# Clustered attention and two FFNs on one core: the weights' rounding moved behind the next gh, b made positive in the lead, the last pair's closing parts spread, the second FFN's outs three units behind

## The chip, the cores and the metric

The kernel runs on one core of a Trainium2 chip. The metric is the device time of one execution in microseconds (us); shown are three runs of the kernel before, of which the median counts. The trace is that of one further, profiled execution. The core's engines each work through their own instructions in order and wait for one another by semaphores: TensorE (PE, the matmuls), VectorE (DVE), ScalarE (ACT), GpSimd (POOL); SyncE (SP) issues the DMAs.

## The reference

Three computations in a row; all of it is in float32, and the weights come as float64.

```
q_assign = argmax(q_n . c_n); k_assign = argmax(k_n . c_n)      # cluster of each query and key, 16 clusters
scores   = q k^T / 8 where q_assign == k_assign, else -1e9
attn     = softmax(scores) v                                     # batch 2, 8 heads, seq 768, head_dim 64
x        = attn as 1536 tokens x 512

h = x @ w_in;  g = max(h, 0) + log1p(exp(-|h|));  x = g @ w_out  # first FFN, 512 -> 2048 -> 512

h = x @ w2_in                                                    # second FFN
g = (a0 + a1 h + a2 h^2 + a3 h^3) / (1 + |b0| |h| + |b1| h^2 + 1e-6)
out = g @ w2_out
```

## The kernel before

**Attention.** Two heads make a pair, and there are eight pairs (NP) with six tiles of 128 keys (NT). Pair 0 is prepared in a lead before the steps; step j then has PE compute the scores of pair j (tile `st`, L320 and L321), the row maxima of pair j+1 (`mxs`, L276), and attention times values (`av`). DVE reduces each `mxs` to a column of `mf` (L280); once six columns stand, PE transposes them (`nt`, L288), DVE makes the row `nr` (L290), and a DMA puts it beside the keys. ACT takes the exponential (`et`), POOL adds the tiles up (`ea`). What a step or the lead does comes from tables of positions (`AT`, `LEAD`): every piece is put on an axis with a number, and the pieces are issued by rising number. In the lead `coefficients` (position AB) issues the DMAs of `a_sb` and `b_sb`, the coefficients a and b of the second FFN.

The closing parts of a pair (`finish`) are 0: Ln and Exp of the sums on ACT, 1 to 3: three products on DVE (L385 to L389), 4: the rounding copy to `xh` on ACT (L394) and the rest `xl` on POOL. Those of the last pair run inside the first FFN.

**FFNs.** 1536 tokens make three blocks of 512; the hidden 2048 make 16 chunks of 128; one chunk for one block is a unit, so each FFN has 48 units, numbered 0 to 47 and 48 to 95. A unit is `g_in` (12 matmuls, L474 to L476, into one of four PSUM tiles `h`), the function on ACT and DVE, which leaves g split into a rounded part `gh` (ACT) and a rest `gl` (DVE, L530 or L532), and `g_out` (12 matmuls, called outs below, L545 to L547 or L549 to L551). Every product is three matmuls: high by high, high by low, low by high. The loop over units writes PE's order: outs(i) come one unit after g(i) in the first FFN and two units after it in the second, one more for a block's first chunk.

**Weights.** A chunk's float64 bits are loaded by one DMA (`stage_w`, 1 MB) and decoded by DVE in three passes (first L428, second L434, third L440); ACT rounds the result to `w` (L444, the cast), and DVE subtracts (L447, the rest). Cast and third pass are one piece. The loop takes four such pieces per unit in the first FFN's first block, so one chunk per unit, and from the second FFN's first unit on one piece per unit for the chunks 14 and 15 that are then left. The queue of pieces is served in order; `DE` puts the pieces of the first five chunks into the attention's last two steps (NP-2 and NP-1). At unit 3 ACT takes the absolute value of `b_sb` (L781), which needs its own activation table.

The first FFN's softplus and the Ln and Exp of attention and second FFN lie in different tables of ACT, which are loaded by ACT_TABLE_LOAD rows.

Of the kernel before, what the change touches and what calls it, by code (L numbers as in the profile page):

```python
# [10 lines left out]
F32 = mybir.dt.float32  # L11
# [17 lines left out]
DE = [  # L29
    [-11.7, -5.09, -3.77, -3.71],  # L30
    [-1.97, 0.49, 2.0, 0.04],
    [0.24, -2.3, -0.8, -0.33],
    [5.39, 3.04, 3.81, 10.72],
    [5.38, 8.42, 3.92, 3.46],
]
FN = [1.65, 2.38, 4.34, 7.01]
LEAD = dict(F1=[-0.92, -0.47], D=-8.72, E1=-2.11, E2=-1.3, OT=0.68, F2=[0.92, 3.97], F3=[3.64, 5.6], F4=[10.75, 6.7],
# [4 lines left out]
def clustered_attention_two_ffns(  # L42
# [372 lines left out]
    def decode_w(f, c):  # L415
# [35 lines left out]

        pieces.extend(((f, c), x) for x in (first, second, third, fourth))

    def run_pieces(n=0, upto=None):

        while pieces and (n > 0 or upto and pieces[0][0] <= upto):
            pieces.pop(0)[1]()
            n -= 1

# [116 lines left out]
    with tc.manual_schedule():  # L576
# [149 lines left out]
        nu = len(units)  # L726
        ahead = 2
        run_pieces(upto=units[0][::2])
        g_in(*units[0])
        av(NP - 1, NT - 1)  # L730
        run_pieces(upto=units[1][::2])
        g_in(*units[1])
        sums(NP - 1)
        att.close()
        pools["wb"] = ctx.enter_context(tc.tile_pool(name="wb", bufs=1))
        last = pools["wb"].tile([128, 2 * NW], F32R, tag=f"w{KF - 1}", name="last").bitcast(F32)
        last = last[:, 0:2 * S].rearrange("p (a n x) -> p a n x", a=2, n=2)
        evac_av(NP - 1, last[:, 0])
        evac_sums(NP - 1, last[:, 1])
        aps.close()  # L740
        pools["py"] = ctx.enter_context(tc.tile_pool(name="ps4", bufs=1, space=bass.MemoryType.PSUM))
        finish(NP - 1, 0)
        for c in range(8, KF - 1):
            stage_w(0, c)

        outs = [[] for _ in range(nu + 4)]
        for i, (f, blk, c) in enumerate(units):
            outs[i + (1, 2)[f] + (c == 0)].append((f, blk, c))
        F1 = NB * KF
        outs[F1] = outs[F1 - 1] + outs[F1]  # L750
        outs[F1 - 1] = []
        for i in range(nu + 3):
            u = units[i] if i < nu else None
            prev = units[i - 1] if 0 < i <= nu and units[i - 1][0] == 1 else None
            if u:
                if u[1] == 0:
                    run_pieces(upto=(u[0], u[2]))
                if i >= ahead:
                    g_in(*u)
                if i == F1:  # L760
                    nc.scalar.preload_act_table_set("natural_log_exp_and_others")
                act1(*u)
                if u[0] == 0:
                    g_hi(*u)
                    g_lo(*u)
            if prev:
                act3(*prev)
# [12 lines left out]
            if i == 3:  # L780
                nc.scalar.activation(out=b_sb, in_=b_sb, func=AF.Abs)  # L781
                stage_w(0, KF - 1)
                stage_w(1, 0)
            for f, c in ((0, i + len(DE)), (1, i - (NB - 1) * KF - 2)):
                if len(DE) * (f == 0) <= c < KF:
                    decode_w(f, c)
            run_pieces(1 if i >= F1 else 4)
            for o in outs[i]:
                g_out(*o)
                if o[:2] == (0, NB - 1) and o[2] < KF - 1:  # L790
                    stage_w(1, o[2] + 1)

# [41 lines left out]
```

## Time and profile before

| | us |
|---|---|
| median of three runs (824.18 to 826.26) | 824.36 |
| the profiled execution | 825.66 |
| its span in the trace | 823.9 |
| PE busy in the span | 782.0 (95%) |
| DVE busy | 597.9 (73%) |
| ACT busy | 441.5 (54%) |
| POOL busy, all of it before the FFNs | 185.5 (23%) |
| mean granted clock of TensorE | 0.979 of full speed |

A busy share is the mean over stages that have different limits: PE, DVE, ACT and POOL share the attention, and PE, DVE and ACT the FFNs. A full granted clock (1.0) is 2.4 GHz and 0.5 is 1.2 GHz; a value between is a mixture over the stretch. In the timelines a group of like instructions is one row with its count, the time in brackets is how long the engine stood idle before the row, and the name behind the arrow is what ended that.

### The profile page before, as it was taken

Reading aid. Unit: us, or ns where it says so; the run is one execution under the profiler, and the core shown is the slowest. Engines: PE = TensorE matmul, PEld = TensorE weight load, DVE = VectorE, ACT = ScalarE, POOL = GpSimd, SP = SyncE. Lnnn points to the kernel's source line nnn. Section 1 sums busy time; section 2 is a strip of 40 time slices with the busy share of each in tenths; the row PEclk is TensorE's granted clock in tenths of the full one; section 3 lists DMA queues with packets and bytes.
Section 4 is the critical chain, followed back from the end, with each engine's and each line's share of the span. In section 5 each row is a group of like instructions: output and inputs, shape, how many; then the busy total and the mean of one; then the engine's idle time right before and its main releaser. Section 6 shows DMA issues by size and latency. Waiting matters only on the chain.

```text
span 823.9 us, 9126 instructions
## 1 busy us (share of the span) xinstructions
PE 782.0 (95%) x3467; PEld 573.8 (70%) x3468; DVE 597.9 (73%) x759; ACT 441.5 (54%) x626; POOL 185.5 (23%) x103
## 2 busy tenths in 40 slices
PE   6799999999988899999999999979999999999997
PEld 3366565656555677788888887757788788887885
DVE  4888778887885878621112678889998798879886
ACT  3456666765474343331223333366777676667674
POOL 3375988898852000000000000000000000000000
PEclk9699999999999999999999999999999999999999
DMA  4553344424073520000000455410000100010001
GB/s 183 164 149 71 117 127 138 124 65 155 1 307 146 211 103 0 1 1 0 1 1 0 157 201 196 161 52 0 1 1 0 52 1 0 1 52 0 1 1 51
DMA packets 14635, 61.65 MB, mean 75 GB/s; under 512 B 3248, under 2 KB 4368, under 8 KB 10496
## 3 DMA queue, kind: packets, MB, share of 16 engines
q1 hardware_dynamic: 14176, 60.19, 21.7%
q10 hardware_dynamic: 416, 0.89, 0.3%
q8 instruction: 27, 0.44, 0.2%
q14 instruction: 16, 0.13, 0.1%
HBM read 49.32 MB, written 3.15 MB: 64 GB/s over the span
## 4 chain that ended last, share of the span: by engine, by line
PE 60%; DVE 23%; ACT 11%; issue 3%; DMA 2%; ACTq 0%; SPq 0%; DVEq 0%
PE av L342 7%; PE h L475 7%; PE h L476 7%; PE h L474 7%; DVE w L440 5%; PE yp L550 4%; PE yp L551 4%; PE st L320 4%; PE yp L549 4%; ACT w L444 4%; PE mxs L276 3%; PE st L321 3%; DVE w L434 3%; PE yp L546 3%; PE yp L547 2%
## 5 line engine op out<-in xcount | busy, mean ns | idle before, releaser
L476 PE MATMUL h<-xh,w 128*128 128x512 f32 x384 | 152.1, 396 | 0.5 <-DVE w L447 0.5
L474 PE MATMUL h<-xh,w 128*128 128x512 f32 x384 | 151.9, 396 | 0.3 <-ACT w L444 0.3
L475 PE MATMUL h<-xl,w 128*128 128x512 f32 x384 | 152.0, 396 | 0.0
L330 POOL TENSOR_TENSOR ea<-ea,et 128x768 f32<-128x768 f32 x60 | 117.8, 1981 | 24.1 <-ACT et L325 22.2
L280 DVE TENSOR_REDUCE mf<-mxs 128x1 f32<-128x768 f32 x96 | 87.6, 951 | 34.8 <-PE mxs L276 34.1
L530 DVE TENSOR_TENSOR gl<-y,gh 128x512 fp32r<-128x512 f32 x48 | 33.1, 691 | 102.6 <-ACT gh L522 102.6
L325 ACT ACTIVATE et<-st 128x768 f32<-128x768 f32 x96 | 73.3, 812 | 60.3 <-PE st L321 57.4
L444 ACT CAST w<-w 128x1024 fp32r<-128x1024 f32 x32 | 33.6, 1049 | 105.6 <-DVE w L440 105.6
L474 PEld LDWEIGHTS h<-xh,w 128*128 128x128 f32 x384 | 72.2, 188 | 19.0 <-issue 1.2
L476 PEld LDWEIGHTS h<-xh,w 128*128 128x128 f32 x384 | 72.1, 188 | 18.1 <-DVE w L447 1.0
L475 PEld LDWEIGHTS h<-xl,w 128*128 128x128 f32 x384 | 72.2, 188 | 17.1
L546 PE MATMUL yp<-gl,w 128*128 128x512 f32 x192 | 78.2, 407 | 4.3 <-DVE gl L530 3.9
L545 PE MATMUL yp<-gh,w 128*128 128x512 f32 x192 | 77.3, 403 | 4.6 <-issue 3.2
L549 PE MATMUL yp<-w,gh 128*128 128x512 f32 x192 | 77.1, 401 | 4.1 <-ACT gh L524 4.0
L550 PE MATMUL yp<-w,gl 128*128 128x512 f32 x192 | 77.7, 405 | 3.3 <-DVE gl L532 3.3
L547 PE MATMUL yp<-gh,w 128*128 128x512 f32 x192 | 76.7, 399 | 0.0
L551 PE MATMUL yp<-w,gh 128*128 128x512 f32 x192 | 76.4, 398 | 0.0
L320 PE MATMUL st<-qt,kt 128*128 128x384 f32 x192 | 70.7, 368 | 4.8 <-ACT et L325 2.4
L487 ACT ACTIVATE y<-h 128x512 f32<-128x512 f32 x48 | 28.5, 595 | 84.0 <-PE h L476 84.0
L342 PE MATMUL av<-et,vr 128*64 128x384 f32 x384 | 71.7, 500 | 1.0 <-ACT et L325 1.0
L321 PE MATMUL st<-qt,kt 81*128 81x384 f32 x192 | 65.7, 342 | 0.0
L447 DVE TENSOR_TENSOR w<-w,w 128x1024 fp32r<-128x1024 f32 x32 | 39.2, 1225 | 32.9 <-ACT w L444 32.9
(122 smaller groups left out, 1319.5 us busy)
## 6 DMA issues: line engine op xcount, KB each, us to landing
w<-in_moe_w SPq DMA_DIRECT2D x32, 1024.0 KB, 4.9
rawx<-in_x SPq DMA_DIRECT2D x7, 768.0 KB, 6.4
rawy<-in_y SPq DMA_DIRECT2D x7, 768.0 KB, 6.4
vr<-in_v SPq DMA_DIRECT2D x8, 384.0 KB, 6.0
kt<-kt SPq DMA_DIRECT2D x7, 384.0 KB, 4.0
out<-yo SPq DMA_DIRECT2D x9, 256.0 KB, 2.5
kt<-qt SPq DMA_DIRECT2D x7, 288.0 KB, 4.0
out<-y SPq DMA_DIRECT2D x3, 256.0 KB, 4.1
```

Source lines behind the costliest of these rows:

```text
L320: nc.tensor.matmul(t[:, n, 0:HS], lhsT=KT[j % 3][:, 0, h, c], rhs=QT[j % 3][:, 0, h, r], start=True, stop=False)
L321: nc.tensor.matmul(t[:, n, 0:HS], lhsT=KT[j % 3][0:RM + 1, 1, h, c], rhs=QT[j % 3][0:RM + 1, 1, h, r], start=False, stop=True)
L330: eng.tensor_tensor(out=ea[j, h], in0=et[j, 0, h] if kt == 1 else ea[j, h], in1=e, op=ALU.add)
L342: nc.tensor.matmul(av_t[j][64 * h:64 * h + 64, n, 0:HS], lhsT=VR[j % 2][:, h, kt, :], rhs=et[j, kt, h][:, n, :], start=kt == 0, stop=kt == ...
L474: nc.tensor.matmul(t, lhsT=wh[:, kk, :], rhs=h, start=kk == 0, stop=False)
L475: nc.tensor.matmul(t, lhsT=wh[:, kk, :], rhs=l, start=False, stop=False)
L476: nc.tensor.matmul(t, lhsT=wl[:, kk, :], rhs=h, start=False, stop=kk == KD - 1)
L546: nc.tensor.matmul(t, lhsT=wh[:, s], rhs=gl, start=False, stop=False)
L547: nc.tensor.matmul(t, lhsT=wl[:, s], rhs=gh, start=False, stop=last)
L549: nc.tensor.matmul(t, lhsT=gh[:, s], rhs=wh, start=first, stop=False)
L550: nc.tensor.matmul(t, lhsT=gl[:, s], rhs=wh, start=False, stop=False)
L551: nc.tensor.matmul(t, lhsT=gh[:, s], rhs=wl, start=False, stop=last)
```

## The change

Nothing that is computed changes. The closing parts, weights and units of both FFNs are put on one axis of positions, as the steps of the attention are, with a table `FT`. On it:

- The decode of a chunk has five pieces instead of four: the cast is its own piece, placed at 1.15 and the rest at 1.25 after the unit in which the three DVE passes stand, which is behind the next unit's `gh` and `gl`. In the second FFN the pieces of chunks 14 and 15 stand in two units each (`D2`).
- `b_sb` is made positive on DVE in the lead, right behind the issue of its DMA; ACT's Abs at unit 3 goes.
- Unit 1's `g_in` comes before unit 0's, both before the last `av` and the sums; the softplus of units 0 and 1 come before the last pair's Ln and Exp; the closing parts stand at positions 0.66, 1.12, 3.35, 5.33 and 9.13.
- The outs of the second FFN come three units behind, from its first chunk on.
- `DE` has five columns and other places.

```
 DE = [
-    [-11.7, -5.09, -3.77, -3.71],
...
+    [-11.88, -5.68, -3.02, -3.84, -4.46],
...
-FN = [1.65, 2.38, 4.34, 7.01]
+FT = dict(G=[-8.44, -11.09, 1.12], AV=-5.78, SM=-1.04, EV=[-1.36, -0.96], FN=[0.66, 1.12, 3.35, 5.33, 9.13],
+    A=[-0.02, 0.22, 1.25], L=[0.26, 0.77, 1.61], D2=[[51.2, 51.8, 52.2, 52.4, 52.8], [56.2, 56.8, 57.2, 57.4, 57.8]])
...
+        def fourth():
             wt[f, c] = slot(f, c, F32R)
             nc.scalar.copy(wt[f, c][:, 0:NW], w32[f, c])
-        def fourth():
+        def fifth():
...
+    def decode(f, c, put, *pos):
+        ps = []
+        def nth(x):
+            if not x:
+                run_pieces(upto=(f, c - 2))
+                ps.extend(decode_w(f, c))
+            run_piece(ps[x])
+        for x, d in enumerate((0.22, 0.3, 0.35, 1.15, 1.25)):
+            put(pos[x] if x < len(pos) > 1 else pos[0] + d, lambda x=x: nth(x))
...
             nc.sync.dma_start(out=b_sb, in_=pb.unsqueeze(0).to_broadcast([128, 2]))
+            nc.vector.scalar_tensor_tensor(out=b_sb, in0=b_sb, scalar=-1.0, in1=b_sb, op0=ALU.mult, op1=ALU.max)
...
-            outs[i + (1, 2)[f] + (c == 0)].append((f, blk, c))
...
-            if i == 3:
-                nc.scalar.activation(out=b_sb, in_=b_sb, func=AF.Abs)
...
+        for c in range(len(DE), KF):
+            decode(0, c, put, c - len(DE))
+        for c in range(KF):
+            decode(1, c, put, *(FT["D2"][c - KF + 2] if c >= KF - 2 else [(NB - 1) * KF + 2 + c]))
+        for i, u in enumerate(units):
...
+            put(FT["G"][i] if i < len(FT["G"]) else i, g)
+            if f == 0:
+                put(FT["A"][i] if i < len(FT["A"]) else i + 0.1, lambda u=u: (act1(*u), g_hi(*u)))
+                put(FT["L"][i] if i < len(FT["L"]) else i + 0.2, lambda u=u: g_lo(*u))
+            else:
...
+                put(i + 0.02, lambda u=u: act1(*u))
+                put(i + 1.03, lambda u=u: (act3(*u), g_hi(*u)))
+                put(i + 0.05, lambda u=u: act2(*u, 0))
+                put(i + 1.06, lambda u=u: g_lo(*u))
+                put(i + 0.07, lambda u=u: act2(*u, 1))
...
+            put(F1 + 0.8 + 0.01 * (i - F1) if F1 - 2 <= i < F1 else i + (1 + (c == 0), 3)[f] + 0.9, o)
```

**DVE in the lead.** `mf0` holds the first pair's row maxima, one column per tile and head; these five belong to the second head; `nr` follows PE's transpose of them. Before:

```order
L280 TENSOR_REDUCE mf0_111<-mxs_347 128x1
L280 TENSOR_REDUCE mf0_111<-mxs_351 128x1
L280 TENSOR_REDUCE mf0_111<-mxs_355 128x1
L280 TENSOR_REDUCE mf0_111<-mxs_359 128x1
L280 TENSOR_REDUCE mf0_111<-mxs_365 128x1
L290 TENSOR_SCALAR nr_377<-nt_375 6x128
```

After:

```order
L281 TENSOR_REDUCE mf0_111<-mxs_347 128x1
L281 TENSOR_REDUCE mf0_111<-mxs_351 128x1
L281 TENSOR_REDUCE mf0_111<-mxs_355 128x1
L281 TENSOR_REDUCE mf0_111<-mxs_359 128x1
L678 SCALAR_TENSOR_TENSOR b_sb_72<-b_sb_72 128x2
L281 TENSOR_REDUCE mf0_111<-mxs_366 128x1
L291 TENSOR_SCALAR nr_378<-nt_376 6x128
```

The new instruction on `b_sb` stands between the fourth and the fifth of the five reductions, so the fifth, the transpose on PE and `nr` stand behind it and behind the DMA that fills `b_sb`.

**ACT at the first FFN's start.** `last` and `r0` belong to the last pair's sums, `y` and `gh` to units 0, 1 and 2 in order of their appearance below (after: units 0 and 1 first, then 2). Before:

```order
L382 ACTIVATE r0_2196<-last_2194 128x768
L383 ACTIVATE r0_2196<-r0_2196 128x768
L487 ACT_TABLE_LOAD
L487 ACTIVATE y_2218<-h_2152 128x512
L522 CAST gh_2220<-y_2218 128x512
L444 CAST w4_2225<-w32_2143 128x1024
L487 ACTIVATE y_2231<-h_2169 128x512
L522 CAST gh_2233<-y_2231 128x512
L444 CAST w3_2239<-w32_2228 128x1024
L487 ACTIVATE y_2258<-h_2245 128x512
L522 CAST gh_2260<-y_2258 128x512
L444 CAST w5_2266<-w32_2242 128x1024
```

After:

```order
L510 ACT_TABLE_LOAD
L510 ACTIVATE y_2221<-h_2170 128x512
L545 CAST gh_2223<-y_2221 128x512
L447 CAST w3_2227<-w32_2148 128x1024
L510 ACTIVATE y_2232<-h_2157 128x512
L545 CAST gh_2234<-y_2232 128x512
L383 ACT_TABLE_LOAD
L383 ACTIVATE r0_2215<-last_2208 128x768
L384 ACT_TABLE_LOAD
L384 ACTIVATE r0_2215<-r0_2215 128x768
L447 CAST w5_2257<-w32_2230 128x1024
L447 CAST w4_2259<-w32_2132 128x1024
```

Softplus and `gh` of units 0 and 1 moved ahead of Ln and Exp, each of which now has a table load of its own ahead of it; two casts and a third load stand ahead of unit 2's softplus.

**DVE in two units of the first FFN's first block** (`gl` closes a unit's function; `w6`, `w7`, `w8` are weight chunks). Before:

```order
L434 SCALAR_TENSOR_TENSOR w32_2331<-w7_1997,w32_2331 128x1024
L530 TENSOR_TENSOR gl_2362<-y_2359,gh_2361 128x512
L440 SCALAR_TENSOR_TENSOR w32_2331<-w7_1997,w32_2331 128x1024
L447 TENSOR_TENSOR w7_2366<-w32_2331,w7_2366 128x1024
L428 TENSOR_SCALAR w32_2369<-w8_2204 128x1024
L434 SCALAR_TENSOR_TENSOR w32_2369<-w8_2204,w32_2369 128x1024
L530 TENSOR_TENSOR gl_2400<-y_2397,gh_2399 128x512
```

After:

```order
L553 TENSOR_TENSOR gl_2324<-y_2321,gh_2323 128x512
L429 TENSOR_SCALAR w32_2329<-w8_2194 128x1024
L450 TENSOR_TENSOR w7_2326<-w32_2275,w7_2326 128x1024
L435 SCALAR_TENSOR_TENSOR w32_2329<-w8_2194,w32_2329 128x1024
L388 SCALAR_TENSOR_TENSOR r0_2215<-last_2208,r0_2215 128x768
L441 SCALAR_TENSOR_TENSOR w32_2329<-w8_2194,w32_2329 128x1024
L553 TENSOR_TENSOR gl_2363<-y_2360,gh_2362 128x512
```

The subtraction (L447, now L450) stood right behind the third pass of the same chunk; now the next unit's `gl` and the next chunk's first pass stand between them.

## Rows read from the trace of the kernel before

**Rows 1.** Waits of PE: releaser; us in total, times, longest us.

```profile
PE yp L549 <- ACT gh L524: 4.0, 3, 2.2
...
PE yp L546 <- DVE gl L530: 3.9, 8, 1.3
...
PE yp L550 <- DVE gl L532: 3.3, 6, 1.6
...
PE yp L545 <- issue: 3.2, 1, 3.2
```

**Rows 2.** Busy time by stretches: length, engines' busy us, TensorE clock, DMA share, GB/s.

```profile
20.00:40.00 20.00, 14.23 (x49) 7.24 (x49) 17.82 (x21) 9.20 (x10) 8.00 (x5) 0.67 0.59 165
...
262.00:300.00 38.00, 29.85 (x107) 22.01 (x108) 27.99 (x30) 17.45 (x23) 1.86 (x1) 0.91 0.57 235
...
343.00:541.20 198.20, 197.03 (x844) 157.90 (x843) 87.36 (x99) 59.21 (x92) 0.00 (x0) 1.00 0.22 79
...
541.20:637.20 96.00, 91.29 (x375) 71.07 (x374) 87.96 (x127) 69.79 (x107) 0.00 (x0) 0.96 0.01 3
```

**Rows 3.** Timeline of PE, two neighbouring units: start, us, instruction, count.

```profile
800.97 0.40 PE L474 MATMUL h<-xh,w 128*128 128x512 f32 x1
...
806.51 0.40 PE L474 MATMUL h<-xh,w 128*128 128x512 f32 x1
```

**Rows 4.** Timeline of DVE in the lead; brackets hold idle time before a row.

```profile
35.39 4.38 DVE L280 TENSOR_REDUCE mf<-mxs 128x1 f32<-128x768 f32 x5
```

**Rows 5.** Timeline of PE in the lead.

```profile
39.82 0.37 PE L288 MATMUL nt<-ident,mf 128*6 128x128 f32 x1
...
42.66 0.95 PE L276 MATMUL mxs<-kt,qt 80*128 80x384 f32 x4 [0.49 <-DMA qt<-mr]
```

**Rows 6.** Timeline of SP's queue in the lead.

```profile
43.02 0.43 SPq L654 DMA_DIRECT2D b_sb<-in_moe_b  x1
```

**Rows 7.** DMA issues: KB each, median us to landing.

```profile
b_sb<-in_moe_b SPq DMA_DIRECT2D x1, 1.0 KB, 2.6
```

**Rows 8.** Timeline of PE in the attention's last steps.

```profile
213.92 0.44 PE L320 MATMUL st<-qt,kt 128*128 128x384 f32 x1 [1.67 <-DVE mf L280]
...
233.68 0.44 PE L320 MATMUL st<-qt,kt 128*128 128x384 f32 x1 [2.10 <-ACT et L325]
```

**Rows 9.** Timeline of DVE in the first FFN.

```profile
265.17 0.69 DVE L530 TENSOR_TENSOR gl<-y,gh 128x512 fp32r<-128x512 f32 x1 [7.36 <-ACT gh L522]
...
265.78 1.22 DVE L440 SCALAR_TENSOR_TENSOR w<-w,w 128x1024 uint32<-128x1024 uint32 x1
...
269.25 0.69 DVE L428 TENSOR_SCALAR w<-w 128x1024 uint32<-128x1024 uint32 x1
...
274.91 1.23 DVE L447 TENSOR_TENSOR w<-w,w 128x1024 fp32r<-128x1024 f32 x1 [1.11 <-ACT w L444]
...
340.19 0.68 DVE L530 TENSOR_TENSOR gl<-y,gh 128x512 fp32r<-128x512 f32 x1
```

**Rows 10.** Timeline of ACT at the first FFN's start.

```profile
262.54 1.28 ACT L487 ACT_TABLE_LOAD   x1
...
263.83 0.60 ACT L487 ACTIVATE y<-h 128x512 f32<-128x512 f32 x1
```

**Rows 11.** Timeline of ACT at the second FFN's start.

```profile
541.83 1.05 ACT L444 CAST w<-w 128x1024 fp32r<-128x1024 f32 x1 [3.88 <-DVE w L440]
```

**Rows 12.** Timeline of PE at the second FFN's start and 16 units on.

```profile
541.37 0.39 PE L474 MATMUL h<-xh,w 128*128 128x512 f32 x1
...
637.20 0.39 PE L474 MATMUL h<-xh,w 128*128 128x512 f32 x1
```

**Rows 13.** Timeline of DVE at the second FFN's start.

```profile
550.45 2.48 DVE L562 TENSOR_TENSOR xl<-yp,xh 128x512 fp32r<-128x512 f32 x4
```

**Rows 14.** Timeline of ACT at a block's end.

```profile
650.23 0.78 ACT L494 ACTIVATE y<-h,a_sb 128x512 f32<-128x512 f32 x1 [3.76 <-DMA out<-y]
```

**Rows 15.** Timeline of PE before the last outs.

```profile
816.57 0.50 PE L549 MATMUL yp<-w,gh 128*128 128x512 f32 x1 [1.48 <-ACT gh L524]
```

More of the change, by code (lines that the diff above doesn't have):

```diff
@@ L450, in fourth, with run_piece @@
             )
-        pieces.extend(((f, c), x) for x in (first, second, third, fourth))
+        new = [[(f, c), x] for x in (first, second, third, fourth, fifth)]
+        pieces.extend(new)
+        pieces.sort(key=lambda p: p[0])
+        return new
+    def run_piece(p):
+        if p[1]:
+            fn, p[1] = p[1], None
+            fn()
     def run_pieces(n=0, upto=None):
         while pieces and (n > 0 or upto and pieces[0][0] <= upto):
-            pieces.pop(0)[1]()
-            n -= 1
+            n -= pieces[0][1] is not None
+            run_piece(pieces.pop(0))
+    def decode(f, c, put, *pos):
[7 more added lines that the diff above has]
+            put(pos[x] if x < len(pos) > 1 else pos[0] + d, lambda x=x: nth(x))
     def weights(f, c, part):
@@ L726, in clustered_attention_two_ffns @@
         nu = len(units)
[L727 to L747, printed above, removed]
-            outs[i + (1, 2)[f] + (c == 0)].append((f, blk, c))
-        F1 = NB * KF
-        outs[F1] = outs[F1 - 1] + outs[F1]
-        outs[F1 - 1] = []
@@ L752, in clustered_attention_two_ffns, with put, last_evac @@
[L752 to L755, printed above, removed]
+        F1 = NB * KF
+        seq = []
+        def put(pos, fn):
+            seq.append((pos, len(seq), fn))
+        last = []
+        def last_evac(n):
+            if n == 0:
+                last.append(last_tile())
+                evac_av(NP - 1, last[0][:, 0])
+            else:
+                evac_sums(NP - 1, last[0][:, 1])
+                aps.close()
+                pools["py"] = ctx.enter_context(tc.tile_pool(name="ps4", bufs=1, space=bass.MemoryType.PSUM))
@@ new lines, in last_tile @@
+        def last_tile():
+            att.close()
+            pools["wb"] = ctx.enter_context(tc.tile_pool(name="wb", bufs=1))
+            for c in range(8, KF - 1):
+                stage_w(0, c)
+            t = pools["wb"].tile([128, 2 * NW], F32R, tag=f"w{KF - 1}", name="last").bitcast(F32)
+            return t[:, 0:2 * S].rearrange("p (a n x) -> p a n x", a=2, n=2)
+        put(FT["AV"], lambda: av(NP - 1, NT - 1))
+        put(FT["SM"], lambda: sums(NP - 1))
+        for x in range(2):
+            put(FT["EV"][x], lambda x=x: last_evac(x))
@@ new lines, in clustered_attention_two_ffns, with rest, g @@
+        for part in range(5):
+            put(FT["FN"][part], lambda part=part: finish(NP - 1, part))
+        def rest():
+            stage_w(0, KF - 1)
+            stage_w(1, 0)
+        put(FT["FN"][4] + 0.01, rest)
+        for c in range(len(DE), KF):
[3 more added lines that the diff above has]
+        for i, u in enumerate(units):
+            f, blk, c = u
+            def g(u=u):
@@ L787, in clustered_attention_two_ffns @@
[L787 to L791, printed above, removed]
+                g_in(*u)
+            put(FT["G"][i] if i < len(FT["G"]) else i, g)
+            if f == 0:
+                put(FT["A"][i] if i < len(FT["A"]) else i + 0.1, lambda u=u: (act1(*u), g_hi(*u)))
+                put(FT["L"][i] if i < len(FT["L"]) else i + 0.2, lambda u=u: g_lo(*u))
+            else:
+                if i == F1:
+                    put(i + 0.01, lambda: nc.scalar.preload_act_table_set("natural_log_exp_and_others"))
+                put(i + 0.02, lambda u=u: act1(*u))
[3 more added lines that the diff above has]
+                put(i + 0.07, lambda u=u: act2(*u, 1))
@@ L794, with o @@
+            def o(u=u):
+                g_out(*u)
+                if u[:2] == (0, NB - 1) and u[2] < KF - 1:
+                    stage_w(1, u[2] + 1)
+            put(F1 + 0.8 + 0.01 * (i - F1) if F1 - 2 <= i < F1 else i + (1 + (c == 0), 3)[f] + 0.9, o)
+        put(F1 + 1.04, lambda: [x() for x in late])
+        for _, _, fn in sorted(seq, key=lambda x: x[:2]):
+            fn()
 _INS = ["x", "y", "v", "centroids", "moe_w", "moe2_w", "moe2_a", "moe2_b"]
```

34 lines of the change are left out of this document (4 added, 30 removed).

## The prediction, made before the change was run

> **What bounds the kernel now.** The waits of PE were read first, then the windows with their granted clock, and then the timelines of the stretches in which these two show a loss. PE is the bound almost everywhere; in the FFNs it stands idle for `gh` and `gl` in few places: 4.0, 3.9, 3.3 and 3.2 us by releaser [rows 1]. The windows show where: of the 38 us from 262 on, PE is busy 29.85, at a mean clock of 0.91; of the 96 us from 541.2 on, 91.29 at 0.96; in the 198.2 us between, all but 1.2 us at 1.00 [rows 2]. So idle time costs twice: after some gaps the clock falls from 2.4 to 1.2 GHz, and matmuls take twice their time. Undisturbed, a unit takes 806.51-800.97 = 5.54 us, both halves of it 2.77 [rows 3]; that is the floor in the FFNs, and what the change can win is the time above it.
>
> **The sum, part by part.** It is made against the profiled execution's 825.66 us, 1.30 above the median of 824.36; the differences are taken over to the median.
>
> *b in the lead: +8.0.* DVE does five row maxima in one run from 35.39 to 39.77 [rows 4]; the transpose on PE follows at 39.82 and PE goes on with scores at once; its next wait is one of 0.49 us at 42.66, for a DMA [rows 5]. In the changed order the operation on `b_sb` stands ahead of the fifth maximum. It waits for a DMA which SP issues at 43.02 only, behind other transfers that the change does not move [rows 6], and which lands 2.6 us later [rows 7], at 45.6. Behind it on DVE stand the fifth maximum, a fifth of 4.38 us = 0.9, and then the transpose: 45.6+0.2+0.9 = 46.7 instead of 39.82, 6.9 later. PE takes its instructions in order, so all scores behind the transpose, which don't need it, are late too. 0.5 of this is taken from the wait at 42.66: 6.4. PE stands idle for about 7 us then, and I add 1.6 for a lower clock behind it: around the 3.2 us idle at the first FFN's start [rows 1] the window shows 0.91 over 38 us, a loss of 0.09 x 38 = 3.4 us, part of it from other gaps; the lead's clock is poor already, 0.67 from 20 to 40 [rows 2], so there is less to lose. No cover is in sight, as PE was the bound before and behind this place. Bounds: 5 (no loss by clock, and more waits for DMAs that swallow the delay) to 9.5.
>
> *The attention's last two steps: -0.8.* `DE` moves decode work. PE's gap of 2.10 at 233.68, where the exponential stands behind a cast that waits for DVE, goes; the gap of 1.67 at 213.92 behind a row maximum moves to another place [rows 8], and by the order after one of about 2.2 stands there. Gain 2.4, losses 0.5 to 1.6; -0.8, bounds +1.5 and -2.4.
>
> *Start and first block of the first FFN: -6.7.* Until chunk 15 is decoded, DVE goes through one chunk per unit: `gl` 0.69, third 1.22, a wait of 1.11 for the cast, subtraction 1.23, first 0.69, second like the third [rows 9]; the instructions overlap a little, and the twelve units between the `gl` at 265.17 and the one at 340.19 take 75.0 us, 6.25 each. Without the wait for the cast (it is placed behind the next `gh`, when DVE has other work), and with what remains at most 5.1 per unit, DVE falls below PE's 5.54: 12 x 5.54 = 66.5, a gain of 8.5. Part of it is the visit of `b_sb` to ACT at unit 3, which costs two table loads of 1.28 [rows 10] and doubles that unit's wait. From the 8.5 I take 1.1, because `gl` of unit 0 is later by the new order (two softplus and the closing Ln and Exp stand otherwise), and 0.7 for closing parts that meet the decode: -6.7, bounds -4.5 and -7.5. The changed order has three loads at this place where two went: one ahead of Ln, one ahead of Exp, one ahead of unit 2's softplus. They lie behind `gh` of unit 1; unit 2's `gl` comes 3 x 1.28 later by them, and that stands against the outs of units 0 and 1 on PE, 5.5 us.
>
> The row shows what a load costs: it starts at 262.54, and the operation behind it at 263.83, 1.29 us in all [rows 10]. The Trainium skill ("ScalarE: Activation LUTs", What ACT_TABLE_LOAD costs) gives about 2.66 us for a switch, 1.28 for the load and 1.38 to drain the engine; by that the three loads would take 8.0 instead of 3.9 us, and this part would be -2.6. The trace of before does not bear the second half out, and I go by the row.
>
> *Third block of the first FFN: -1.8.* There DVE waits for the cast in each unit again; PE lost 1.2 us in the window from 343 [rows 2], and each gap slows the matmul behind it a little. With the cast behind the next `gh`, and the same sum of DVE work, it goes: bounds -1.2 and -2.1.
>
> *Start of the second FFN: -5.8.* The first activation of unit 48 stands on ACT behind a cast that waited 3.88 us for DVE [rows 11]. From the second unit's `g_in` at 541.37 to that of unit 65 at 637.20, 95.8 us [rows 12] hold 31 half units, 31 x 2.77 = 85.9: 9.9 lost. With outs three units behind, PE has one more `g_in` and one more outs ahead of the first `gl`. What stays: the four late `xl`, 2.48 us in a row on DVE [rows 13], and chunks 14 and 15, whose five pieces stand in two units each now, where one piece per unit stood; in the unit with third pass, wait and subtraction DVE has 1.2+1.1+1.2 = 3.5 us on top of its own seven instructions (4.9, at 0.7 each, as `gl` [rows 9]) and falls behind 5.54. Walking along the order, PE waits about 0.2 at the outs of unit 48 and 2.2 at those of 52, and 1.6 for the clock behind it: 4.0 of the 9.9 stay. Bounds -2 (the clock stays low as before) and -9.6.
>
> *Block ends: -2.4.* At a block's end ACT waits 3.76 us for the store of an output tile [rows 14], and PE runs dry. From 637.20 [rows 12] to 806.51 [rows 3] lie 30 units; 30 x 5.54 = 166.2 of 169.3 us, so 3.1 are lost at both ends together. One more outs in reserve, 2.8 us on PE and with it the `g_in` between, covers most of it. Bounds -1.2 and -3.1.
>
> *End: -2.1.* The last outs wait for `gh`, 1.48 us [rows 15], and twice about 0.25 for `gl`. So the way from the last `h` to `gl` is about 2.0 longer than the two outs (5.5) that PE has meanwhile, 7.5; three outs are 3 x 2.77 = 8.3 and cover it. Bounds -1.5 and -2.2.
>
> Nothing is put down for the buffers. `gh` and `gl` have three each: `gh` of unit i+3 needs the outs of unit i done, and stands on ACT behind the first activation of unit i+4, which waits for a `g_in` that PE does after those outs.
>
> Sum: 8.0-0.8-6.7-1.8-5.8-2.4-2.1 = -11.6. 824.4-11.6 = 812.8.
>
> **The rivals.** *1. The wait in the lead costs next to nothing*, because later waits of the attention on DMAs and on POOL swallow it, or the DMA is down earlier. For it: PE waits for DMAs in the lead. Against it: from 46 on PE's bracketed waits are few, and DMAs all move along. Without the 8.0, and with 1.0 for the operation itself and a rest of the wait, 824.4-19.6+1.0 = 805.8. *2. DVE stays the bound in the FFNs*: closing parts and chunks 14 and 15 meet `gl`, and half of the two large terms (6.7 and 5.8) is lost: 812.8+6.2 = 819. For it: the 4.9 us of DVE in a unit of the second FFN leave 0.6 for decode. Against: it has slack of a unit more. *3. A drain of ACT's tables* as in the rule above: +4.1, 816.9; the row at 262.54 speaks against it. *4. Slower: the idle 7 us in the lead leave the clock at half until the attention runs evenly.* For it: the clock was 0.67 from 20 to 40, with PE busy 14.23 of 20 us [rows 2], so in the lead it does not come back by itself. Price: what PE has to do from 46.7 on takes twice its time, 1 us lost for each us of work; the 1.6 are in the sum, and from 12+ us on top, that is from about 14 us of work at half clock, it decides; with 17 us, 828. Against: after 3.2 us of idle time the clock was back inside the same 38 us. That the change does not do what it says is no rival here, as the order shows each move.
>
> The Trainium skill ("TensorE: Matmul & The Clock Gate", What's actually happening) calls the low clock the default that activity releases; by that the price ends once PE is kept busy, which speaks against rival 4. The windows here agree as far as the clock is 1.00 in the 198 us after the low one.
>
> **The numbers.** Forecast 0.57, rival 1 0.14, rival 2 0.18, rival 3 0.04, rival 4 0.04, other mishaps 0.03. The forecast's own terms, with bounds of 1 to 3 us each that partly cancel, give 809 to 816. To hold eight in ten the range reaches to rivals 1 and 2: 804.5 to 820. A difference under 0.3%, 2.5 us, can hardly be told from no change: faster below 821.9, 0.88; within, 0.06; slower above 826.8, 0.06.
>
> **What would show it.** Right: an idle of 6 to 7 us on PE ahead of the transpose `nt` near 40, ended by DVE, with DVE waiting for the DMA of `b_sb`; `gl` one per 5.5 us from unit 2 on and no idle ahead of DVE's subtraction; no row for `b_sb` on ACT; at the last outs no wait; one PE wait of about 2 us near the fifth unit of the second FFN. Wrong: a PE gap near 40 under 3 us (rival 1); DVE at a pitch near 6 in the first FFN, or several PE waits for `gl` in the second (rival 2); a gap of over 2 us on ACT around a table load (rival 3); a clock below 0.7 from 45 to 60 (rival 4).

## The result, and the profile after

The changed kernel takes 816.56 us (median of four runs, 813.68 to 817.65) against 824.27 us of the kernel before: a ratio of 0.9898, 95% interval 0.9867 to 0.9929, so about 8 us or 1.0% faster. Forecast were 812.8 us, from 804.5 to 820. The way and the range held; the gain was two thirds of the 11.6 us forecast. The profiled execution took 817.65 us (span 815.9), the slowest of the four, 8.0 below that of the kernel before.

Where the 8.0 us come from is read from the times at which PE reaches the same work in both traces. The kernel before: one of pair 6's maxima, the first `g_in`, `g_in` of units 3, 17 and 67, and the last matmul (unit 49 is in [rows 12]).

```profile
172.28 0.97 PE L276 MATMUL mxs<-kt,qt 80*128 80x384 f32 x4 [0.54 <-ACT et L325]
...
250.13 0.39 PE L474 MATMUL h<-xh,w 128*128 128x512 f32 x1
...
274.94 0.50 PE L474 MATMUL h<-xh,w 128*128 128x512 f32 x1 [0.26 <-ACT w L444]
...
360.22 0.39 PE L474 MATMUL h<-xh,w 128*128 128x512 f32 x1
...
645.58 0.39 PE L474 MATMUL h<-xh,w 128*128 128x512 f32 x1
...
819.70 0.39 PE L551 MATMUL yp<-w,gh 128*128 128x512 f32 x1
```

The changed kernel, the same seven places (units 3, 17, 49 and 67 behind the first `g_in`):

```profile
179.23 0.97 PE L277 MATMUL mxs<-kt,qt 80*128 80x384 f32 x4 [0.53 <-ACT et L326]
...
260.09 0.39 PE L497 MATMUL h<-xh,w 128*128 128x512 f32 x1
...
284.59 0.40 PE L497 MATMUL h<-xh,w 128*128 128x512 f32 x1
...
362.62 0.39 PE L497 MATMUL h<-xh,w 128*128 128x512 f32 x1
...
541.11 0.39 PE L497 MATMUL h<-xh,w 128*128 128x512 f32 x1
...
639.92 0.39 PE L497 MATMUL h<-xh,w 128*128 128x512 f32 x1
...
811.71 0.39 PE L574 MATMUL yp<-w,gh 128*128 128x512 f32 x1
```

The difference grows to +6.95 by the first row and +9.96 by the second, then falls: +9.65, +2.40, -0.26, -5.66, and -7.99 at the last matmul. By stretch, against the terms of the sum:

| stretch | forecast | profiled |
|---|---|---|
| lead (b) | +8.0 | +6.9 |
| attention's last steps | -0.8 | +3.0 |
| first FFN, to unit 17 | -6.7 | -7.6 |
| first FFN, to unit 49 | -1.8 | -2.7 |
| second FFN, to unit 67 | -5.8 | -5.4 |
| block ends and end | -2.4-2.1 | -2.3 |
| sum | -11.6 | -8.0 |

In this execution two terms are off by 3.8 and 2.2 us, the others by about 1 each.

PE's waits after (as [rows 1]):

```profile
PE nt L289 <- DVE mf L281: 11.1, 2, 6.7
...
PE yp L569 <- DVE gl L553: 2.9, 1, 2.9
...
PE mxs L277 <- DVE mf L281: 2.4, 1, 2.4
...
PE yp L572 <- ACT gh L547: 2.3, 2, 1.6
...
PE yp L572 <- DVE yo L596: 2.0, 1, 2.0
```

The waits of [rows 1] for `gl` and `gh` have shrunk to 2.9 and 2.3 us. New are 11.1 for the transpose `nt` in the lead (one of its two waits stood there before, 4.2 us) and 2.0 for `yo`, a copy of an output tile. Now the windows with their granted clock, before:

```profile
40.00:60.00 20.00, 18.98 (x95) 13.29 (x95) 15.52 (x19) 11.54 (x15) 14.54 (x8) 0.97 0.52 144
...
200.00:245.00 45.00, 39.69 (x201) 24.14 (x198) 39.38 (x31) 26.20 (x34) 30.77 (x16) 0.96 0.45 181
```

and after (as [rows 2]):

```profile
40.00:60.00 20.00, 12.94 (x61) 9.79 (x61) 10.76 (x14) 8.44 (x9) 8.43 (x4) 0.74 0.17 36
...
200.00:245.00 45.00, 39.05 (x180) 22.36 (x179) 32.65 (x29) 19.07 (x27) 34.70 (x18) 0.89 0.25 93
...
262.00:300.00 38.00, 33.67 (x135) 25.11 (x134) 34.79 (x36) 21.56 (x26) 1.81 (x1) 0.91 0.47 194
...
541.20:640.00 98.80, 96.03 (x410) 76.34 (x409) 92.78 (x134) 72.20 (x113) 0.00 (x0) 1.00 0.02 6
```

From 40 to 60 the clock fell from 0.97 to 0.74 and PE's busy time from 18.98 to 12.94 us; from 200 to 245, the attention's last steps, it is 0.89 instead of 0.96. The start of the first FFN, though it begins 10 us later, is busier (33.67 of the 38 us against 29.85) at the same 0.91, and the second FFN's first 99 us are at 1.00, where [rows 2] had 0.96.

The lead went as forecast, row by row. DVE waits for the DMA, as [rows 4 to 7] let expect:

```profile
45.37 0.16 DVE L678 SCALAR_TENSOR_TENSOR b_sb<-b_sb 128x2 f32<-128x2 f32 x1 [7.09 <-DMA b_sb<-in_moe_b]
```

and PE for the row maximum behind it, at 46.45 where 46.7 was forecast and 39.82 stood [rows 5]:

```profile
46.45 0.38 PE L289 MATMUL nt<-ident,mf 128*6 128x128 f32 x1 [6.69 <-DVE mf L281]
```

At the first FFN's start (as [rows 9]) DVE's subtraction of chunk 3 waits 2.05 us for its cast, and `gl` of unit 0 stands behind it:

```profile
273.92 1.23 DVE L450 TENSOR_TENSOR w<-w,w 128x1024 fp32r<-128x1024 f32 x1 [2.05 <-ACT w L447]
...
275.67 0.69 DVE L553 TENSOR_TENSOR gl<-y,gh 128x512 fp32r<-128x512 f32 x1
```

PE waits for that `gl`, and the matmul of 0.79 us, where 0.40 is usual, shows the clock at 1.2 GHz behind the gap; it stays there until 282.3:

```profile
276.41 0.79 PE L569 MATMUL yp<-gl,w 128*128 128x512 f32 x1 [2.89 <-DVE gl L553]
```

### The profile page after: what moved, and what is told of

Its sections match the earlier page's. It is cut to its first block, busy times and chain, and to the rows that moved or that the text cites. A ratio compares the mean times of both kernels' runs of the same rounds, so it can differ in the third digit from the quotient of the medians.

```text
span 815.9 us, 9120 instructions
## 1 busy us (share of the span) xinstructions
PE 774.9 (95%) x3468; PEld 573.9 (70%) x3468; DVE 596.7 (73%) x760; ACT 443.2 (54%) x626; POOL 186.6 (23%) x103
## 4 chain that ended last, share of the span: by engine, by line
PE 73%; DVE 15%; ACT 7%; DMA 2%; issue 1%; POOL 1%; SPq 0%; ACTq 0%; POOLq 0%; DVEq 0%
PE h L498 9%; PE h L499 9%; PE h L497 9%; PE av L343 7%; PE yp L569 5%; PE yp L570 5%; PE yp L568 5%; PE st L321 4%; PE yp L572 4%; PE yp L573 4%; PE yp L574 4%; PE st L322 3%; PE mxs L277 3%; ACT et L326 2%; DVE y L531 2%; DVE y L539 2%
## 5 line engine op out<-in xcount | busy, mean ns | idle before, releaser
L572 PE MATMUL yp<-w,gh 128*128 128x512 f32 x192 | 75.7, 394 | 4.3 <-ACT gh L547 2.3
L573 PE MATMUL yp<-w,gl 128*128 128x512 f32 x192 | 75.8, 395 | 0.5 <-DVE gl L555 0.5
L574 PE MATMUL yp<-w,gh 128*128 128x512 f32 x192 | 75.5, 393 | 0.0
L277 PE MATMUL mxs<-kt,qt 80*128 80x384 f32 x192 | 52.9, 385 | 11.3 <-DMA kt<-mr 4.8
L321 PEld LDWEIGHTS st<-qt,kt 128*128 128x128 f32 x192 | 36.8, 192 | 24.8 <-DVE mf L281 7.1
```

What stands on the lines that cost most here:

```text
L321: nc.tensor.matmul(t[:, n, 0:HS], lhsT=KT[j % 3][:, 0, h, c], rhs=QT[j % 3][:, 0, h, r], start=True, stop=False)
L572: nc.tensor.matmul(t, lhsT=gh[:, s], rhs=wh, start=first, stop=False)
L573: nc.tensor.matmul(t, lhsT=gl[:, s], rhs=wh, start=False, stop=False)
L574: nc.tensor.matmul(t, lhsT=gh[:, s], rhs=wl, start=False, stop=last)
```

## The experiments

All times are medians; ratios are to the kernel before in the same set of runs, in which it took 823.7 to 825.0 us. The changed kernel's own ratio is 0.9898; 0.001 is 0.8 us.

**b made positive behind the first attention step**

```
-            nc.vector.scalar_tensor_tensor(out=b_sb, ...)        # in coefficients()
...
             step(j)
+            if j == 0:
+                nc.vector.scalar_tensor_tensor(out=b_sb, in0=b_sb, scalar=-1.0, in1=b_sb, op0=ALU.mult, op1=ALU.max)
```

> The changed kernel, with the operation that makes b positive issued behind the first attention step instead of in the lead. Theory (the wait for the DMA of b_sb in the lead holds back PE by the 6.7 us that the trace shows and nothing later swallows it): PE's transpose nt near 40 comes at about 39.8 again, no wait of 6.7 ahead of it, and the time falls by 6.5 to 7.5 us against the changed kernel, to about 809.5. Rival (the delay in the lead is partly made up elsewhere, as the attention's last steps and the first FFN's start wait for weights that come no earlier): under 4 us of the 6.7 come back.

Measured: 807.03 us, 0.9788 (0.9770 to 0.9807), 9.1 us below the changed kernel by the ratios. The wait ahead of `nt` is gone and its cost came back: the rival (under 4) is refuted. The two intervals leave about 3 us either way, so that 9.1 does not contradict the theory's 6.5 to 7.5. Windows of this kernel, for comparison with those above:

```profile
40.00:60.00 20.00, 18.25 (x94) 12.24 (x92) 15.85 (x19) 11.61 (x14) 15.32 (x9) 1.00 0.53 150
...
200.00:245.00 45.00, 39.34 (x198) 24.30 (x197) 39.96 (x30) 25.09 (x33) 33.00 (x16) 0.96 0.41 166
```

The clock from 200 to 245 is 0.96 again, although PE's gaps there are those of the changed kernel; the longest of them, 2.44 us there:

```profile
224.38 0.62 PE L277 MATMUL mxs<-kt,qt 80*128 80x384 f32 x2 [2.42 <-DVE mf L281]
```

So the two profiled executions differ in what follows a gap: 0.07 of 45 us is 3.1 us, about the 3.0 of the attention's last steps. (The window cuts the two traces at different work; from pair 7's first maxima to the first `g_in` in both, the clock is 0.97 against 0.91, which is 3.4 us.)

**The first pass over chunk 1 back behind the row maxima**

```
-    [-2.84, 0.47, 3.51, -4.55, 4.5],
+    [-1.97, 0.47, 3.51, -4.55, 4.5],
```

> The changed kernel, with one number of DE put back: the first pass over chunk 1 stands behind the step's last four row maxima again instead of among them. Theory (this pass, at 1.97 us beside POOL, makes the row maxima late, and PE waits 2.44 us for one at 232.2 and then runs at 1.2 GHz up to 238.7): the wait at 232 goes or falls under 0.7, the low clock behind it too, and 2.5 to 5 us are won, 812 to 814. Rival (the third closing part, 2.58 us beside POOL in the same place, is what makes them late, and it stays): under 1.5 us won, a wait of over 1.2 stays.

Measured: 816.41 us, 0.9902 (0.9872 to 0.9932): no difference that can be told. The trace shows the theory's mechanism (no wait of PE near 232 any more), so the place of the first pass was the cause of that wait; the third closing part keeps its place and takes 1.87 us instead of 2.58. But the time did not stay won. The second pass of the chunk takes 2.73 us instead of 1.67, POOL working beside it (14.84 of the 15 us from 230 on):

```profile
229.32 1.87 DVE L390 TENSOR_TENSOR avs<-avs,r 128x768 f32<-128x768 f32 x1
...
235.25 2.73 DVE L435 SCALAR_TENSOR_TENSOR w<-w,w 128x1024 uint32<-128x1024 uint32 x1
```

and 30 us later PE waits for a sum `ea` that DVE adds behind the decode:

```profile
266.29 1.48 PE L366 MATMUL sm<-ea,ones 128*64 128x384 f32 x7 [0.62 <-DVE ea L331]
```

The first `g_in` comes 1.65 us earlier than in the changed kernel's trace, which is no more than executions of the same code differ by (two of the traces below have it 2.1 and 2.2 us earlier without this edit). PE's waits behind it in the first FFN are longer by 0.65, and 1.07 us are left at unit 67; then the wait for `yo` (2.01 us here) has 3.4 us of low clock behind it, which it has not in the changed kernel's trace. The expected 2.5 us were not won by the medians; by the intervals, over 3 us either way, a gain of that size is not excluded.

**Cast and subtraction straight behind the third pass**

```
-        for x, d in enumerate((0.22, 0.3, 0.35, 1.15, 1.25)):
+        for x, d in enumerate((0.22, 0.3, 0.35, 0.351, 0.352)):
```

> The changed kernel, with the cast and the subtraction of a chunk on the axis straight behind its third pass, as in the kernel before. Theory (the wait of 1.11 us for the cast sets DVE's pitch above PE's): DVE waits about 1.1 us per chunk again, pitch 5.9 in blocks 1 and 3 of the first FFN, 6 to 9 us slower, 823 to 826. Rival (what the first block won came from the closing parts' places and from the missing visit of b to ACT): under 3 us slower.

Measured: 837.19 us, 1.0151 (1.0127 to 1.0174), 20.8 us above the changed kernel: the sign as expected, the size more than double, and slower than the kernel before. DVE's timeline, subtractions with their wait and a `gl` between:

```profile
288.36 1.23 DVE L450 TENSOR_TENSOR w<-w,w 128x1024 fp32r<-128x1024 f32 x1 [1.11 <-ACT w L447]
...
289.50 0.68 DVE L553 TENSOR_TENSOR gl<-y,gh 128x512 fp32r<-128x512 f32 x1
...
320.23 1.23 DVE L450 TENSOR_TENSOR w<-w,w 128x1024 fp32r<-128x1024 f32 x1 [1.12 <-ACT w L447]
...
326.31 1.23 DVE L450 TENSOR_TENSOR w<-w,w 128x1024 fp32r<-128x1024 f32 x1 [1.12 <-ACT w L447]
```

The wait of 1.11 is back, and the pitch is 326.31-320.23 = 6.08 us against PE's 5.54. The profiled execution, 834.74 us, is the fastest of the four and 17.1 us above the changed kernel's. The pitch accounts for about 12 x 0.54 = 6.5 us in the first block (unit 3 to 17 took 90.7 us, in the changed kernel 78.0), and the stretch to unit 49 for 2.6. The rest, which no run separates: 4.27 us that PE waits for the `gl` at 289.50 with a low clock behind it for 6 us, and a start of the second FFN as in the kernel before (gaps of 2.23 and 1.57 us at 564 to 567, low clock to 572.8; 4.2 us more to unit 67).

**Outs of the second FFN two units behind**

```
-            ... else i + (1 + (c == 0), 3)[f] + 0.9, o)
+            ... else i + (1, 2)[f] + (c == 0) + 0.9, o)
```

> The changed kernel, with the second FFN's outs two units behind again (three for a block's first chunk). Theory by the trace (three units behind covers the end, about 2.5 us, and the units with chunks 14 and 15, and costs the 2.00 us that PE waits at the first block's end for an output tile's copy on DVE): slower by 1 to 4 us, with the 1.5 us wait ahead of the last outs back, and the wait for DVE's copy near 645 gone. Rival (what the second FFN won is the decode's spread alone): same time within 1 us.

Measured: 822.46 us, 0.9975 (0.9961 to 0.9989), 6.3 us above the changed kernel, more than expected. The wait for `yo` is gone, but PE waits in more places for `gh` and `gl`:

```profile
PE yp L572 <- ACT gh L547: 5.4, 6, 1.5
...
PE yp L573 <- DVE gl L555: 1.6, 6, 0.4
```

Against 2.3 and 0.5 us in two places each. In the trace 2.8 us are lost between units 49 and 67 and 3.2 behind, 6.0 of the 7.7 us that the change won there. The gain in the second FFN is thus the distance of the outs above all, and three units are worth more than one end of the program.

**The first outs of a block one more behind**

```
-            ... else i + (1 + (c == 0), 3)[f] + 0.9, o)
+            ... else i + (1, 3)[f] + (c == 0) + 0.9, o)
```

> The changed kernel, with the outs of each block's first chunk in the second FFN one unit further behind (four). Theory (at a block's end the first outs of the next block need an output tile of PSUM back; its copy stands on DVE, which runs some units late, and PE waits 2.00 us for it; one g_in more between gives 2.8 us): the wait near 645 goes, the first outs at 52 wait less too, and 1 to 3 us are won, 813.5 to 815.5. Rival (ACT's wait of 4.29 us for the store of the output tile delays gh as well, so another wait takes its place): under 0.7 us.

Measured: 814.84 us, 0.9867 (0.9837 to 0.9896), 2.6 us below the changed kernel by the ratios and 1.7 by the medians; the two intervals overlap. In the trace the wait for `yo` is gone, and of the two for `gh` one is left:

```profile
PE yp L572 <- ACT gh L547: 1.8, 1, 1.8
```

From unit 67 to the end of the last matmul the changed kernel took 172.2 us, this one 170.0. The traces of the five later kernels with this edit have 170.0 to 170.1 there and that of b late, without it, 172.2, so these 2.2 us are the edit's. That the second wait for `gh` went is not shown to be: with b late alone it is missing too.

**Three gl ahead of Ln and Exp**

```
-FT = dict(G=[-8.44, -11.09, 1.12], ...
-    A=[-0.02, 0.22, 1.25], L=[0.26, 0.77, 1.61], ...
+FT = dict(G=[-8.44, -11.09, -0.5], ...
+    A=[-0.02, -0.01, 0.0], L=[-0.015, -0.005, 0.005], ...
```

> The changed kernel, with softplus, gh and gl of units 0, 1 and 2 ahead of all rounding of chunk 3 and ahead of the last pair's Ln and Exp (four positions changed; one table load fewer). Theory (gl of unit 0 stands on DVE behind the subtraction of chunk 3, which waits 2.05 us for its cast; PE waits 2.89 us for that gl and then runs at 1.2 GHz for 5 us): the wait of 2.89 falls under 0.8, g_in of unit 3 starts 19 to 21 us after that of unit 1 instead of 24.5, and 3 to 5 us are won. Rival (what PE gains there it loses at the outs of unit 2 to 4, since chunks 3 to 5 and Ln and Exp come later): under 1.5 us won.

The edit changes six positions, not four. Measured: 821.17 us, 0.9942 (0.9918 to 0.9966): 3.6 us slower than the changed kernel. The trace has as many table loads as the changed kernel's, not one fewer. The rival held, and more. The wait of 2.89 is gone and unit 3 comes 20.7 us behind the first `g_in` instead of 24.5. But then ACT waits for a chunk to be decoded, with the table load and unit 3's softplus behind that cast:

```profile
289.89 1.04 ACT L447 CAST w<-w 128x1024 fp32r<-128x1024 f32 x1 [5.42 <-DVE w L441]
...
290.96 1.28 ACT L510 ACT_TABLE_LOAD   x1
```

and PE for that unit's `gh`, with 4.6 us at 1.2 GHz behind the gap:

```profile
293.55 0.80 PE L568 MATMUL yp<-gh,w 128*128 128x512 f32 x1 [4.32 <-ACT gh L545]
```

DVE is nearly full here (34.79 of the 38 us from 262 on in the changed kernel): moving PE's wait does not make the decode faster.

**One part of the change alone: b in the lead of the kernel before**

```
             nc.sync.dma_start(out=b_sb, in_=pb.unsqueeze(0).to_broadcast([128, 2]))
+            nc.vector.scalar_tensor_tensor(out=b_sb, in0=b_sb, scalar=-1.0, in1=b_sb, op0=ALU.mult, op1=ALU.max)
...
-                nc.scalar.activation(out=b_sb, in_=b_sb, func=AF.Abs)
```

> The kernel before, with one part of the change alone: b is made positive on DVE in the lead, and ACT's Abs at unit 3 goes with its two table loads. Theory: 6.9 us lost at the transpose in the lead, up to 3 more or less by the clock behind it, and 2 to 3 us won in unit 3, where DVE's wait for the cast falls from 2.22 to 1.11 and the next gh comes earlier: 826.5 to 831. Rival (the kernel before has slack in the attention that swallows the delay): under 825.

Measured: 834.43 us, 1.0097 (1.0067 to 1.0127), 8.0 us slower than the kernel before (the edge of the expected range is passed by the median). The delay in the lead is real and not swallowed. At the maxima near 172 this trace is 9.1 us late, not 6.9, with the same wait of 6.8 ahead of `nt`; the clock from 40 to 60 is lower than in the changed kernel's trace:

```profile
40.00:60.00 20.00, 13.25 (x55) 11.03 (x56) 9.24 (x11) 6.54 (x8) 7.29 (x4) 0.64 0.10 27
```

From the first `g_in` to unit 17 it takes 109.5 us, the kernel before 110.1: ACT's visit to b had cost next to nothing there, not the 2 to 3 us expected.

**Four edits together**: b late, chunk 1's pass late, first outs one more behind, three `gl` ahead.

> The changed kernel with four edits of these experiments together: b made positive behind the first attention step, the first pass over chunk 1 late, first outs of a block one more behind, and three gl before Ln. If the parts add up (9.5 from the first as measured, 0 to 1.7, 1 to 3, 3 to 5): 798 to 803. If the waits found take each other's place: 803.5 to 807.

Measured: 809.18 us, 0.9808 (0.9771 to 0.9845). By the ratios of the four edits alone the sum is 0.9898-0.0110+0.0004-0.0031+0.0044 = 0.9805: the parts add up, the three `gl` as a loss.

**Two edits together**: b late and the first outs one more behind.

> The changed kernel with the two edits that won most by themselves: b made positive behind the first attention step (9.5 us), and first outs of a block one more behind (about 2). If they add up: 804 to 806. Rival (the one more behind wins only where the lead's delay shifts the clock): 807 and over.

Measured: 806.09 us, 0.9778 (0.9753 to 0.9803). Against 0.9788 with b alone this is no difference that can be told; the intervals overlap. The wait for `yo` is gone; in this execution a gap of 1.76 us at 565 has 3 us of low clock behind it.

**Cast and subtraction of chunks 14 and 15 a unit later**, with the two edits.

```
-    ... D2=[[51.2, 51.8, 52.2, 52.4, 52.8], [56.2, 56.8, 57.2, 57.4, 57.8]])
+    ... D2=[[51.2, 51.8, 52.2, 53.4, 53.5], [56.2, 56.8, 57.2, 58.4, 58.5]])
```

> As the kernel with these two edits, and cast and subtraction of chunks 14 and 15 one unit later, so that DVE does not wait for the cast in the unit of the third pass. Theory (that wait of 1.11 us and the subtraction in one unit make DVE late by 3.5 us, and PE waits 1.6 to 1.8 us for gh, at times with 1.2 GHz behind it for 3 us): the wait near 563 falls under 0.6, 1 to 3 us won against the kernel with two edits. Rival (DVE is late by the sum of its work, wherever the pieces stand): the wait is only pushed one unit on, under 0.7 us won.

Measured: 804.56 us, 0.9774 (0.9752 to 0.9796). The wait went as the theory said, from 1.76 to 0.56, and no low clock follows it:

```profile
568.60 0.50 PE L572 MATMUL yp<-w,gh 128*128 128x512 f32 x1 [0.56 <-ACT gh L547]
```

A second wait, 0.50, stands at 597.77, one unit behind the one that the changed kernel has beside chunk 15. By the medians 1.5 us are won, by the ratios 0.3; by the times it can't be told from none. In the traces the stretch from unit 49 to 67 takes 97.6 us, with the two edits alone 98.9.

**And the first pass over chunk 1 late**, with the three edits.

> As the kernel with three edits (b late, outs, cast a unit later), and the first pass over chunk 1 behind the row maxima. By the trace of the same edit alone the wait of 2.4 us in step NP-2 goes and 0.4 and 0.6 us come elsewhere: 1 to 2 us won against the kernel with three edits, more where the gap is followed by 1.2 GHz. Rival (the time lost there is made up by waits for weights at the first FFN's start in any case): same within 0.7 us.

Measured: 804.08 us, 0.9758 (0.9742 to 0.9774), the fastest kernel of this study: 20 us below the kernel before and about 12 below the changed one. The last edit's own share, 0.5 to 1.3 us, is within the uncertainty.

**One table load fewer**, with the two edits.

```
             put(FT["FN"][part], lambda part=part: finish(NP - 1, part))
+        put(FT["FN"][0] - 0.01, lambda: nc.scalar.preload_act_table_set("natural_log_exp_and_others"))
```

> As the kernel with two edits, and the table that holds both Ln and Exp loaded ahead of the last pair's Ln, so that Exp needs no load: one ACT_TABLE_LOAD fewer, 1.28 us by the row. Theory (at the first FFN's start DVE's decode sets the pace, not ACT): same within 0.7 us of the kernel with two edits. Rival (a load stands on the path to unit 2's gl, and costs 1.3, or 2.7 with a drain): 1.2 to 2.7 us won.

Measured: 805.30 us, 0.9777 (0.9759 to 0.9795), the same as with two edits, 0.9778. ACT's timeline of this kernel, with one load for Ln and Exp:

```profile
264.67 1.28 ACT L783 ACT_TABLE_LOAD   x1
...
265.96 0.85 ACT L383 ACTIVATE r<-last 128x768 f32<-128x768 f32 x1
...
266.84 0.84 ACT L384 ACTIVATE r<-r 128x768 f32<-128x768 f32 x1
```

The changed kernel's, with two:

```profile
275.05 1.28 ACT L383 ACT_TABLE_LOAD   x1
...
276.35 0.84 ACT L383 ACTIVATE r<-last 128x768 f32<-128x768 f32 x1
...
277.21 1.28 ACT L384 ACT_TABLE_LOAD   x1
```

Each operation starts 1.29 to 1.30 us after its load began. The intervals would leave room for 1.3 us, but from the first `g_in` to unit 17 this trace takes 102.2 us and that of the two edits 102.3: the load is off the path.

## Why the prediction was right, and where not

The direction was right, and so were most of the mechanisms; a third of the forecast gain did not come.

*Right: b in the lead.* Forecast +8.0; 6.9 in the changed kernel's trace, 9.1 when this part is made alone, 8.0 by that part's ratio, and 9.1 back when it is taken away. Rival 1, that the wait is absorbed, is refuted by both runs. Rival 4 (the clock stays low) is so in a mild form only: 0.74 and 0.64 from 40 to 60, 1.00 from 60 on. Over the window that its sign named, 45 to 60, it was 0.82 in the changed kernel's trace and 0.69 with b alone, which just meets the sign; but there half clock ended near 54, and the 14 us of work at half clock that it needed to decide did not come.

*Right: the first FFN.* -6.7 and -1.8 forecast, -7.6 and -2.7 in the trace; of the 2.7, 1.5 fall before unit 48 and 1.1 between the `g_in` of units 48 and 49, which no term covered. With the cast beside the third pass the wait of 1.11 us and a pitch of 6.08 are back and 20.8 us are lost, more than the 8.5 of the step; so the step had the cause, and what the edit costs at the start and in the second FFN stands outside it. The sign that no idle stands ahead of DVE's subtraction did not come: there were 2.05 us at chunk 3, and 0.93, 0.39 and 0.56 at three later ones. The step counted 12 units at the steady pitch, and took part of the gain as due to b's visit to ACT; the run with b alone gives that part as about 0.6.

*Right: the second FFN's start.* -5.8 forecast, -5.4 in the trace. Of the two waits forecast, the 2.2 at the outs of unit 52 came as 1.55, in this trace without the low clock put down behind it; the 0.2 at those of unit 48 did not come, and one of 0.76 at those of unit 57, beside chunk 15, was not foreseen. The run with the cast a unit later shows that the wait for the cast was most of the first.

*Wrong: "Block ends: -2.4".* Together with the end, which was right (no wait ahead of the last outs; from unit 95's `g_in` to the last matmul 2.5 us less, the one more outs taken off), this came to -2.3 instead of -4.5. The step saw the outs in reserve cover ACT's wait for the store, and they do; it missed that with a flat distance of three the first outs of the next block follow the last outs of this one with one `g_in` between, where the kernel before had two, and need their PSUM tile back; its paragraph on buffers counts `gh` and `gl` only. The copy that frees the tile stands on DVE behind work of older units, and DVE is still late there from the decode of chunks 14 and 15: a unit's `gl` starts 18.3 us behind its `g_in` at unit 60, 14.7 at 63 and 10.6 from 75 to 81. With outs two units behind, where PE waits in more places, it is 10.6 at 63. So the copy starts 3.98 us behind the last outs, in the kernel before and with outs two behind 1.31:

```profile
642.07 0.69 DVE L555 SCALAR_TENSOR_TENSOR gl<-y,gh 128x512 fp32r<-128x512 f32 x1
...
644.06 0.68 DVE L596 COPY yo<-yp 128x512 f32<-128x512 f32 x1
```

and PE waits for it:

```profile
644.89 0.47 PE L572 MATMUL yp<-w,gh 128*128 128x512 f32 x1 [2.00 <-DVE yo L596]
```

At the second block's end the distance is the same, but DVE has caught up: the copy starts 1.31 us behind the outs, which end at 731.47, and PE does not wait.

```profile
732.78 0.68 DVE L596 COPY yo<-yp 128x512 f32<-128x512 f32 x1
```

With one unit more for these outs the wait is gone and 2.2 us from unit 67 to the end are won. The 3.1 us that the term took for lost were too much as well: in the kernel before PE's gaps between units 65 and 95 sum to 1.05 us, and the kernel with the first outs one more behind, which has no gap there, still takes 793.71-626.44 = 167.3 us where the term put 166.2 (a unit takes up to 5.60 us behind a block's start). So about 2.0 could be won; in the changed kernel the stretch takes 169.5 us, as long as the 169.3 before.

*Wrong in part: "The attention's last two steps: -0.8".* +3.0 in this trace, outside the bounds of that term. The gap of 2.1 that was forecast is there (2.10 at 213.70); a second, 2.44 at 232.18, was not foreseen: the first pass over chunk 1 stands among the last row maxima, and taking it out of there removes the gap. The bigger part is not the gaps: with one of 0.96 they sum to 5.5 us, and in the kernel before to 5.1 ([rows 8], 0.96 and 0.34). What differs is the clock, 0.89 from 200 to 245 against 0.96, which is 3.1 us. In the kernel with b late the gaps are the same to 0.03 us, the clock is 0.96, and from the maxima near 172 to the first `g_in` it takes only 0.3 us more than the kernel before. So the gaps cost 1.1 more than the term said, within its bounds, and the price of low clock behind them, for which it had no share, was missing. That price changes between executions of the same program: the changed kernel's four runs have 817.65, 816.59, 813.68 and 816.52 us at a mean clock of 0.972, 0.971, 0.978 and 0.973. Four of the experiments leave the code up to the first `g_in` as it is in the changed kernel. With the cast straight behind the third pass, the outs two behind, the first outs one more behind and three `gl` ahead, this stretch takes -1.3, +2.3, -1.2 and +2.3 us against the kernel before, and the delay at the maxima near 172 is 9.0, 6.9, 9.1 and 7.5 us. (With b alone, in the order of the kernel before, the stretch takes -0.8.) With the first outs one more behind the same gaps (2.09, 2.33, 0.96) have no low clock behind them:

```profile
181.37 0.97 PE L277 MATMUL mxs<-kt,qt 80*128 80x384 f32 x4 [0.54 <-ACT et L326]
...
200.00:245.00 45.00, 39.18 (x202) 23.89 (x201) 38.12 (x32) 22.42 (x31) 37.56 (x18) 1.00 0.31 115
...
257.98 0.39 PE L497 MATMUL h<-xh,w 128*128 128x512 f32 x1
```

So -0.8 lies within what the same code gives, and the +6.9 and +3.0 of the table are one execution's division. By the first `g_in` the five traces are 7.8 to 10.0 us late, where the forecast had +7.2 for both terms. Which gaps get the low clock in a given execution stays open.

Rival 2 (DVE stays the bound) holds for the first FFN's start only, where DVE is busy 34.79 of 38 us and the run with three `gl` first gained nothing. Rival 3, a drain beside a table load, is refuted by the rows and by the run with one load fewer. The Trainium skill ("ScalarE: Activation LUTs", What ACT_TABLE_LOAD costs) counts 1.38 us of drain on top of 1.28; no row here shows the 1.38.

## What to carry to other kernels

An operation that costs 0.16 us cost 7 to 9 here when it was queued, on an engine whose next result PE needs, ahead of a DMA's landing: before moving an instruction, look up what lands when, and what stands behind it in its queue. A longer distance between producer and consumer lets an engine between them stay late while PE goes on, and whatever else that engine does in program order (here the copy that frees a PSUM tile, at the first block's end) is late too. A wait removed from PE was not won where another engine was full in that stretch, as DVE at the first FFN's start. And one trace prices a gap by its own execution's clock: compare the same stretch in several traces of the same code before calling a term wrong.

## What was not expected of the hardware

The same gap costs differently. With gaps of 2.1, 2.3 to 2.4 and 1.0 us in the attention's last steps the clock from 200 to 245 was 0.89 in the changed kernel's trace, 0.96 with b late and 1.00 with the first outs one more behind, with the same instructions around them; after the 6.7 to 6.8 us in the lead the stretch from 40 to 60 ran at 0.74 or 0.64, and the delay at 172 was 6.9 or 9.1 us accordingly. And DVE's second pass took 1.2 us wherever POOL was idle, and at chunk 1, beside POOL's additions, 1.67 us in the changed kernel and 2.73 us with the first pass late.
